# Zero products in TensorE's gaps, a weight's sign by Prelu, and a new order of work

## The chip, the cores and the metric

The kernel runs on one core of one Trainium2 chip. The metric is the device time of one execution in microseconds (us). Five engines work side by side: TensorE (products, PE in the profile, its weight loads PEld), VectorE (DVE), ScalarE (ACT), GpSimd (POOL) and SyncE (SP), whose queue issues the DMAs.

## The reference

Three stages follow one another. Linear attention over 4 batches, 8 heads, 576 tokens, head size 64, with 128 random features; an MLP of 512 - 2048 - 512 with a leaky ReLU; and an MLP of 512 - 1024 - 512 with a softmax-weighted product and a layer norm inside.

```python
def phi(x):
    proj = np.einsum('bhsd,md->bhsm', x, omega)
    h = proj - np.sum(x * x, axis=-1, keepdims=True) / 2.0
    h = h - np.max(h, axis=-1, keepdims=True)
    return np.exp(h) / np.sqrt(m)
q_p, k_p = phi(q * scale), phi(k * scale)
kv = np.einsum('bhsm,bhsd->bhmd', k_p, v);  z = np.sum(k_p, axis=2)
attn = einsum(q_p, kv) / (einsum(q_p, z) + 1e-06)      # -> x: 2304 tokens x 512
h = x @ w_in;   x = np.maximum(0.01 * h, h) @ w_out
h = x @ w2_in;  e = np.exp(h - h.max());  solu = h * e / e.sum()
out = ((solu - mean) / np.sqrt(var + 1e-06) * g_ln) @ w2_out
```

q, k, v and omega come as float32. The four weight matrices come as float64, so each element is two 32-bit words and the kernel must rebuild a float32 from them.

## The kernel before, in words

The 2304 tokens are 18 tiles of 128. For a tile of k (`k_unit`) the kernel loads the rows of all heads, transposes them, multiplies by omega, takes the maximum and the exponential, and adds the products with v to the batch's sum kv (two PSUM tiles, `kv0` and `kv1`, for even and odd heads). For a tile of q (`q_unit`) it computes the same features and multiplies them with kv of the batch. Two tiles make a block of 256 tokens for the first MLP: `st1` is its first layer (product at L1080 for the first block in float32, at L1086 for the others in split float16), `st2` its second (L1126 and L1130). `mlp2_in` (L1245), `mlp2_mid` and `mlp2_out` (L1319) are the second MLP.

A weight matrix comes in pieces of 128 x 512 float64 (`piece`, L359). Each has a buffer `wraw` (four of them), a DMA of 512 KB, and then: the high words scaled by 2^-112 into x (L378 on ScalarE, or L381 on POOL; the list `ya` says which), a shift left by three (L384, VectorE), the sign, and the three bits of the low word (L400, VectorE). The sign comes in one of two ways (list `sg`): a Sign on ScalarE (L393) and a product on POOL (L404), or a bit operation on VectorE (L397). The pieces of the first MLP are numbered 0 to 31 (w_in, then w_out), all of the second MLP have 99. Later a piece is cut into two float16 parts (`cut_weight`); the list `wlo` says which are cut with POOL's help.

The first block needs all pieces of w_in in order, four (a chunk) for each two of its eight groups; the cuts come when it is through with them.

The order of all instructions is chosen when the program is built. `Issue` (L28) is a planner: it steps through generators, each with a priority (the smaller, the earlier), and keeps a model of when each engine is free. An operation that is ready goes into its engine's heap; when the engine is free in the model, the operation with the smallest priority is taken and emitted. On the chip each engine then runs its instructions in this order. Buffers are counted: `get` waits for one, `put` gives it back; a waiting `get` is served by priority, but a buffer that is free goes to the first who asks. `X` holds the numbers of buffers, the priorities (`due` of each unit from `deadlines`, plus the offsets in `off`), and the lists that say which engine does what. A weight's load and work have the priority w1 + w1s * chunk (or w2 + w2s * row) + its offset.

`v_bound` reads the v of the last two batches once, at the start, to find a scale, and is started ahead of the units; `v_load` brings v for the sums. Both take a buffer `v`. `omega_prep` loads omega twice, one load after the other, and transposes it (L496).

`warm_up` (L476) is ten products of 512 columns of a zeroed tile at the start of TensorE's work, into a bank that a tile `y` has for this time.

Of the kernel before, what the change touches and what calls it, by code (L numbers as in the profile page):

```python
# [9 lines left out]
F32 = mybir.dt.float32  # L10
F16 = mybir.dt.float16
# [10 lines left out]

X = {'NF': 1, 'bufs': {'qe': 3, 'v': 2, 'qf': 2, 'ke': 4, 'hl': 1, 'x': 2, 'g': 4, 'sg': 1, 'qT': 3, 'x16': 3, 'scr': 2, 'T': 1, 'wraw': 4, 'raw': 1, 'y16': 2, 'lnT': 3, 'l16': 2, 'kf': 2, 'v16': 3}, 't0': -33.903, 'tb': 232.119, 'w1': -284.718, 'w1s': -136.489, 'w2': 138.823, 'w2s': 11.803, 'b0': -432.337, 'b1': 58.985, 'dk': 50.766, 'dq': -11.625, 'dl': 188.956, 'c1': -291.243, 'c2': -74.124, 'pw2': 106.795, 'wlo': [1, 4, 11, 12, 13, 15, 16, 20, 23, 24, 25, 27, 30, 32, 33, 35, 39], 'vd': 829.749, 'warm': 10, 'psq': ['k0', 'k4', 'q4', 'q7', 'q8'], 'ep': ['k1', 'k12', 'k14', 'k16', 'k3', 'k4', 'k5', 'k6', 'k7', 'q0', 'q1', 'q15'], 'te': ['k00', 'k01', 'k10', 'x00', 'x11'], 'KH': [2, 3], 'vb': 346.274, 'ya': [0, 3, 4, 5, 6, 7, 8, 9, 11, 12, 13, 15, 20, 21, 24, 25, 28, 29, 30, 31, 99], 'EK': [0, 1, 2, 3, 6, 7, 8], 'pkv': 346.335, 'tail': 3, 'sg': [1, 3, 9, 11, 13, 14, 18, 19, 20, 29], 'off': {'q1': -191.7, 'w15': 506.92, 'w4': 40.08, 'w23': -275.29, 'w18': -183.5, 'w24': 49.7, 'w28': -14.13, 'q10': 139.42, 'k8': -330.31, 'q5': 145.52, 'w7': 124.91, 'w25': -154.21, 'w12': -66.92, 'w9': -115.28, 'w19': -197.26, 'w31': 261.27, 'w27': -201.22, 'k11': 48.35, 'q16': -139.34, 'w5': 217.6, 'k9': 38.48, 'q2': 183.77, 'w8': 21.25, 'w14': -107.85, 'w30': 145.73, 'e1': 252.86, 'w26': -557.18, 'k13': -105.91, 'q0': 40.51, 'k0': 104.04, 'k7': 50.33, 'q13': 128.56, 'k2': -96.21, 'k16': -192.43, 'w22': 156.65, 'k6': 19.45, 'k4': 269.03, 'q8': 59.66, 'v0': 128.19, 'w20': -694.52, 'w16': 175.72, 'w0': 75.39, 'q6': 56.03, 'v2': -26.38, 'w17': 84.39, 'w13': 306.69, 'w3': 539.5, 'v1': 84.72, 'e2': -21.1, 'w1': -197.63, 'k15': -23.53, 'q3': 335.59, 'w2': 510.76, 'q7': 95.01, 'q4': 199.6, 'w11': 44.31, 'q12': 134.9, 'k5': 117.67, 'q15': -72.68, 'w10': 64.06, 'k14': -24.99, 'w29': 230.81, 'q17': -396.39, 'k12': 87.94, 'v3': -15.84, 'w21': -618.68, 'q11': 42.31, 'q9': 133.04, 'k17': 24.82, 'q14': -332.91, 'k1': 23.08, 'e3': -27.5, 'w6': 222.38, 'k3': 306.64, 'k10': -25.2}, 'pe': -72.358}


class Issue:  # L28
# [152 lines left out]
def linear_attention_moe_kernel(  # L181
# [177 lines left out]
    def piece(src, r0, c0, n, x, pool, nr):  # L359

        yield "get", "wraw"
        u = h = None
        if src.dtype == F32:
            yield "op", "DMA", 1.58, lambda: SP.dma_start(out=x, in_=src[r0:r0 + 128, c0:c0 + n])
        else:
            h = {}

            def load():
                h["r"] = mk(pool, "wraw", [128, n, 2], I32)
                SP.dma_start(out=h["r"].rearrange("p n w -> p (n w)"),  # L370
                             in_=src[r0:r0 + 128, c0:c0 + n].bitcast(I32))
            yield "op", "DMA", 1.58, load

            hw = lambda: h["r"][:, :, 1].bitcast(F32)
            xi = x.bitcast(I32)

            def base_A():
                yield "op", "A", 0.61, lambda: A.activation(out=x, in_=hw(), func=AF.Copy, scale=2.0 ** -112)  # L378

            def base_G():  # L380
                yield "op", "G", 0.75, lambda: G.tensor_scalar(out=x, in0=hw(), scalar1=2.0 ** -112, scalar2=1.0,  # L381
                                                               op0=ALU.mult, op1=ALU.mult)
            yield from either("ya", nr, base_A, base_G)
            yield "op", "V2", 0.38, lambda: V.tensor_scalar(out=xi, in0=xi, scalar1=3, scalar2=None,  # L384
                                                           op0=ALU.logical_shift_left)
            sg = {}

            def sign():
                yield "get", "sg"

                def emit():
                    sg["t"] = mk(pool, "sg", [128, n], F16)
                    A.activation(out=sg["t"], in_=hw(), func=AF.Sign)  # L393
                yield "op", "A", 0.6, emit, True

            def sign_bit():
                yield "op", "V2", 0.62, lambda: V.scalar_tensor_tensor(  # L397
                    out=xi, in0=h["r"][:, :, 1], scalar=-(1 << 31), in1=xi, op0=ALU.bitwise_and, op1=ALU.bitwise_or)
            yield from either("sg", nr, sign, sign_bit)
            yield "op", "V2", 0.62, lambda: V.scalar_tensor_tensor(  # L400
                out=xi, in0=h["r"][:, :, 0], scalar=29, in1=xi, op0=ALU.logical_shift_right, op1=ALU.bitwise_or)

            def signed():
                yield "op", "G", 1.2, lambda: G.tensor_tensor(out=x, in0=x, in1=sg["t"], op=ALU.mult)  # L404
                yield "put", "sg"
            yield from either("sg", nr, signed, lambda: ())
        yield "put", "wraw"

    def bound(pool, x, am, n, gain=1.0):
# [63 lines left out]
            yield "set", ("w2", f)  # L473


    def warm_up():  # L476

        yield "get", "y"
        ps = mk(ps_y, "y", [128, DM], F32)
        z = omT.rearrange("p a m -> p (a m)").bitcast(F16)  # L480
        for n in range(X["warm"]):
            yield "op", "PE", 0.215, lambda: PE.matmul(ps, lhsT=z[:, 0:128], rhs=z, start=True, stop=True), True
        yield "put", "y"

    def omega_prep():
        yield "get", "scr"
# [310 lines left out]
    def k_unit(i, pri):  # L797
# [14 lines left out]
        def half(hh):  # L812
# [12 lines left out]
                yield "wait", ("v", nv)  # L825
            for p, n, b in segs[i]:
                if (yield "nth", ("kv of", b), 1):
                    yield "get", "kv"
                    kv_ps[b] = [ps_kv.tile([128, HH, D + 2], F32, name=f"kv{g}", tag=f"kv{g}") for g in range(2)]
                    yield "set", ("kv at", b)  # L830
                    yield "end",
                yield "wait", ("kv at", b)

                def acc(p=p, n=n, b=b):
                    left["kv", b, hh] -= 1
                    first = left["kv", b, hh] == len(batch_segs[b]) - 1
# [583 lines left out]
```

## Time and profile before

| | us |
|---|---|
| median of 3 runs | 716.52 (715.64 to 718.06) |
| the profiled execution | 716.71 |
| its span, first to last instruction | 714.9 |
| mean granted clock of TensorE in it | 0.982 |

The profiled execution is the one whose rows are shown below. A row "8.00:10.00 2.00, ..." of a view by windows gives for a stretch the busy time of each engine and the count of its instructions, TensorE's granted clock, the busy share of the DMA engines and the GB/s that they moved. A clock of 1.00 is 2.4 GHz, 0.50 is 1.2 GHz. A float32 product of TensorE stands as two records.

### The profile page before, as it was taken

How to read it: one execution, taken by the hardware profiler on the slowest of the kernel's cores; microseconds unless marked ns; L12 is line 12 of the kernel's file. 1: busy time of each engine (PE TensorE's matmuls, PEld its weight loads, DVE VectorE, ACT ScalarE, POOL GpSimd, SP SyncE). 2: the span in 40 equal slices, each digit the busy share in tenths (PEclk: the TensorE clock that was granted, in tenths of full speed). 3: DMA queues.
4: the chain of work that ended last, by engine and by line, in shares of the span. 5: the costliest groups of instructions: out<-in, count | busy, mean ns of one | idle time of the engine just before them, and what ended most of it. 6: DMA issues, size and time to landing. Idle time of an engine off the chain costs nothing. (4 is left out here: it accounts for less than half of the span.)

```text
span 714.9 us, 12932 instructions
## 1 busy us (share of the span) xinstructions
PE 687.9 (96%) x4892; PEld 446.1 (62%) x4892; DVE 493.1 (69%) x1197; ACT 380.4 (53%) x801; POOL 128.0 (18%) x170
## 2 busy tenths in 40 slices
PE   4889989999999999999999999999999999999997
PEld 2878975577677667767677767566654444444443
DVE  5998989889676586765964426974068758668870
ACT  3888868698675766756565526876132121121121
POOL 3321332434210110011110000043001101101120
PEclk7878999999999999999999999999999999999999
DMA  9878786548665345453654516901015233333343
GB/s 281 242 241 284 191 227 141 111 89 163 98 126 89 56 83 115 83 98 73 120 98 66 85 26 219 270 9 30 1 31 91 72 89 72 82 69 74 69 106 76
DMA packets 183598, 81.19 MB, mean 114 GB/s; under 512 B 146416, under 2 KB 175088, under 8 KB 183536
## 3 DMA queue, kind: packets, MB, share of 16 engines
q1 hardware_dynamic: 183536, 80.37, 49.4%
q8 instruction: 38, 0.62, 0.3%
q14 instruction: 24, 0.20, 0.1%
HBM read 41.75 MB, written 4.72 MB: 65 GB/s over the span
## 5 line engine op out<-in xcount | busy, mean ns | idle before, releaser
L1130 PE MATMUL y<-w,g 128*128 128x512 f16 x768 | 177.6, 379 | 0.8 <-DVE g L1104 0.3
L1086 PEld LDWEIGHTS <-w 128*128 128x128 f16 x1536 | 148.6, 98 | 26.9 <-issue 0.6
L1130 PEld LDWEIGHTS <-g 128*128 128x128 f16 x768 | 72.9, 98 | 78.7 <-DVE g L1104 3.7
L1086 PE MATMUL h<-xy,w 128*128 128x256 f16 x960 | 112.3, 273 | 0.0
L1319 PE MATMUL h<-wo,lnT 128*128 128x512 f16 x432 | 95.8, 379 | 0.0
L1104 DVE TENSOR_TENSOR g<-h,g 128x512 f16<-128x512 f32 x64 | 43.8, 685 | 46.8 <-ACT g L1103 46.5
L1245 PE MATMUL h<-wi,xy 128*128 128x512 f16 x336 | 75.3, 379 | 0.0
L1319 PEld LDWEIGHTS <-lnT 128*128 128x128 f16 x432 | 42.3, 98 | 51.0
L1102 ACT ACTIVATE h<-h 128x512 f32<-128x512 f32 x64 | 38.1, 596 | 57.2 <-PE h L1086 57.1
L1086 PE MATMUL h<-xT,w 128*128 128x256 f16 x576 | 68.1, 273 | 0.0
L1274 ACT ACTIVATE e<-h,nb,u 128x1024 f32<-128x1024 f32 x18 | 21.7, 1205 | 74.8 <-DVE nb L1271 64.0
L1245 PEld LDWEIGHTS <-xy 128*128 128x128 f16 x336 | 32.9, 98 | 38.8
L783 ACT ACTIVATE qe<-a,nb,sc 128x128 f32<-128x128 f32 x120 | 44.6, 471 | 15.5 <-DVE nb L774 14.3
L1328 ACT ACTIVATE osb<-h,c_out 128x512 f32<-128x512 f32 x18 | 12.4, 687 | 68.2 <-PE h L1319 36.4
L768 DVE TENSOR_REDUCE mx<-a 128x4 f32<-128x512 f32 x63 | 41.7, 682 | 7.3 <-PE a L761 5.0
L869 POOL TENSOR_SCALAR qf<-qe 128x512 f16<-128x512 f32 x30 | 19.1, 637 | 121.7 <-ACT qe L783 116.0
L1103 ACT ACTIVATE g<-h 128x512 f16<-128x512 f32 x64 | 38.5, 602 | 1.1
L1289 POOL TENSOR_TENSOR rs<-ve,mhalf 128x1 f32<-128x1 f32 x18 | 9.9, 550 | 145.4 <-DVE ve L1288 145.4
L783 ACT ACTIVATE ke<-a,nb,sc 128x128 f32<-128x128 f32 x64 | 23.6, 468 | 17.2 <-DVE nb L774 9.9
L1080 PE MATMUL h<-xT,w 128*128 128x256 f32 x128 | 29.1, 382 | 2.2 <-ACT g L1099 2.2
L872 DVE SCALAR_TENSOR_TENSOR qf<-qe,qf 128x512 f16<-128x512 f32 x30 | 21.9, 729 | 13.6 <-POOL qf L869 13.4
L1126 PE MATMUL y<-w,g 128*128 128x512 f32 x64 | 29.5, 600 | 0.2 <-DVE w L400 0.2
(200 smaller groups left out, 1134.2 us busy)
## 6 DMA issues: line engine op xcount, KB each, us to landing
wraw<-in_moe_w_in_dram SPq DMA_DIRECT2D x24, 512.0 KB, 5.7
wraw<-in_moe_w_out_dram SPq DMA_DIRECT2D x24, 512.0 KB, 4.4
v<-in_v_dram SPq DMA_DIRECT2D x12, 512.0 KB, 5.7
raw<-in_k_dram SPq DMA_DIRECT2D x8, 512.0 KB, 4.6
raw<-in_q_dram SPq DMA_DIRECT2D x8, 512.0 KB, 5.0
out_dram<-osb SPq DMA_DIRECT2D x16, 256.0 KB, 2.2
v<-in_v_dram SPq DMA_DIRECT2D x6, 128.0 KB, 5.1
lnT<-l SPq DMA_TRANSPOSE x36, 3.2
```

What stands on the lines that cost most here:

```text
L768: yield "op", "V", 0.6, lambda: V.tensor_reduce(out=u["mx"][:, hh::2], in_=w["ps"], axis=AX.X, op=ALU.max)
L783: A.activation(out=x[:, h, :], in_=w["ps"][:, h, :], func=AF.Exp, scale=st["sc"], bias=u["nb"][:, 2 * h + hh:2 * h + hh + 1])
L872: yield "op", "V" if stay else "V2", 0.62, lambda: V.scalar_tensor_tensor(out=w["f"][:, :, 1, :], in0=w["e"], scalar=2.0 ** 14, in1=w["f"] ...
L1080: PE.matmul(ps[:, f, :], lhsT=stash(w1, c * KC + kc)[:, o:o + 128], rhs=xT[j][:, kc, :], start=(kc == 0), stop=(kc == KC - 1))
L1086: PE.matmul(ps[:, f, :], lhsT=w1[:, c * KC + kc, w, o:o + 128], rhs=xT[j][:, :, xo + kc, :], start=(n == 0), stop=(n == 3 * KC - 1))
L1102: yield "op", "A", 0.48, lambda: A.activation(out=ps, in_=ps, func=AF.Prelu, scale=2.0 ** -19, alpha=0.01)
L1103: yield "op", "A", 0.48, lambda: A.activation(out=gg[:, 0], in_=ps, func=AF.Copy)
L1104: yield "op", "V", 0.6, lambda: V.tensor_tensor(out=gg[:, 1], in0=ps, in1=gg[:, 0], op=ALU.subtract)
L1126: PE.matmul(y_ps[j][t], lhsT=gg[:, f, ts], rhs=stash(w2, 2 * p + f), start=(ends[0] and f == 0), stop=(ends[1] and f == 1))
L1130: PE.matmul(y_ps[j][t], lhsT=gg[:, a, f, ts], rhs=w2[:, 2 * p + f, w, :], start=(ends[0] and f == 0 and n == 0), stop=(ends[1] and f == 1 ...
L1245: PE.matmul(ps[:, f, :], lhsT=yT[i][:, a + c, :], rhs=W["i"][:, 2 * c + f, w, :], start=(j == 0 and c == 0), stop=(j == 2 and c == KC - 1))
L1319: PE.matmul(ps, lhsT=t[:, a, f, :], rhs=W["o"][:, f, w, :], start=(j == 0 and f == 0), stop=(j == 2 and f == KF2 - 1))
```

## The change

- `X` is new: priorities, offsets, buffers and lists. Of the buffers, v goes from 2 to 1, g 4 to 9, ke 4 to 3, kf 2 to 4, qT 3 to 2, x16 3 to 2, y16 2 to 3, lnT 3 to 2. The last tiles of the second MLP that go ahead of its output layer are 5 instead of 3 (`tail`).
- The list `sg` is gone. Pieces in `ya` (22 of 32) get x and sign in one Prelu on ScalarE; for a negative number its slope of -2^32 sets an exponent bit that the shift by three moves to the sign's place. The others, the second MLP's among them, are scaled on POOL and get the sign by the bit operation on VectorE.
- `warm_up` is now up to 300 products of 128 columns of zeros, with the largest priority number of all, so that one is emitted when nothing else is ready for TensorE in the model. They go to 128 added columns of the tile `kv1`, and stop when the tiles of the attention are all done.

```diff
-X = {... 'bufs': {'qe': 3, 'v': 2, ... 'ke': 4, ... 'g': 4, ... 'lnT': 3, ...}, ... 'w1': -284.718, ... 'w2': 138.823, ... 'warm': 10, ... 'tail': 3, 'sg': [1, 3, 9, 11, 13, 14, 18, 19, 20, 29], ...}
+X = {... 'bufs': {'qe': 3, 'v': 1, ... 'ke': 3, ... 'g': 9, ... 'lnT': 2, ...}, ... 'w1': 54.105, ... 'w2': 352.332, ... 'warm': 300, ... 'tail': 5, ...}
+    nil = const.tile([128, 128], F16, name="nil")
-            yield from either("ya", nr, base_A, base_G)
-            yield "op", "V2", 0.38, lambda: V.tensor_scalar(out=xi, in0=xi, scalar1=3, ...
+            def sign_A():
+                yield "op", "A", 0.63, lambda: A.activation(out=x, in_=hw(), func=AF.Prelu, scale=2.0 ** -112,
+                                                            alpha=-2.0 ** 32)
+                yield from shift()
+            def sign_V():
+                yield "op", "G", 0.75, lambda: G.tensor_scalar(out=x, in0=hw(), scalar1=2.0 ** -112, scalar2=1.0,
+                                                               op0=ALU.mult, op1=ALU.mult)
+                yield from shift()
                 yield "op", "V2", 0.62, lambda: V.scalar_tensor_tensor(
                     out=xi, in0=h["r"][:, :, 1], scalar=-(1 << 31), in1=xi, op0=ALU.bitwise_and, op1=ALU.bitwise_or)
-            yield from either("sg", nr, sign, sign_bit)
+            yield from either("ya", nr, sign_A, sign_V)
...
-                yield "op", "G", 1.2, lambda: G.tensor_tensor(out=x, in0=x, in1=sg["t"], op=ALU.mult)
...
+    idle = []
+    def kv_place(b):
+        ps = [ps_kv.tile([128, HH * (D + 2) + 128], F32, name=f"kv{g}", tag=f"kv{g}") for g in range(2)]
+        kv_ps[b] = [p[:, 0:HH * (D + 2)].rearrange("p (h d) -> p h d", h=HH) for p in ps]
+        idle.append(ps[1][:, HH * (D + 2):])
+
     def warm_up():
-        yield "get", "y"
-        ps = mk(ps_y, "y", [128, DM], F32)
-        z = omT.rearrange("p a m -> p (a m)").bitcast(F16)
+        yield "get", "kv"
+        kv_place(0)
         for n in range(X["warm"]):
-            yield "op", "PE", 0.215, lambda: PE.matmul(ps, lhsT=z[:, 0:128], rhs=z, start=True, stop=True), True
-        yield "put", "y"
+            if not idle:
+                break
+            def zeros(n=n):
+                if idle:
+                    PE.matmul(idle[-1], lhsT=nil, rhs=nil, start=n == 0, stop=False, skip_group_check=True)
+            yield "op", "PE", 0.1, zeros, True
...
+        idle.clear()
...
-        sch.go(warm_up(), -101)
+        sch.go(warm_up(), 1e8)
```

## Rows read from the trace of the kernel before

**Rows 1.** The page's first part: busy us (share of the span) x instructions.
```profile
PE 687.9 (96%) x4892; PEld 446.1 (62%) x4892; DVE 493.1 (69%) x1197; ACT 380.4 (53%) x801; POOL 128.0 (18%) x170
```
**Rows 2.** Windows by stage: busy us (x count) by engine, clock, DMA share, GB/s.
```profile
0.00:70.95 70.95, 54.06 (x349) 47.79 (x350) 57.76 (x132) 50.14 (x118) 18.17 (x28) 0.83 0.87 262
20.00:50.60 30.60, 26.60 (x189) 24.89 (x187) 29.65 (x66) 26.67 (x69) 7.70 (x8) 0.89 0.81 238
70.95:710.50 639.55, 633.84 (x4545) 398.36 (x4543) 435.36 (x1067) 329.62 (x683) 109.79 (x142) 1.00 0.46 98
710.50:714.90 4.40, 0.00 (x0) 0.00 (x0) 0.00 (x0) 0.68 (x1) 0.00 (x0) 0.78 0.26 60
```
**Rows 3.** Waits of TensorE: us in total, times, longest us.
```profile
PE h L496 <- DMA scr<-in_omega_dram: 8.6, 1, 8.6
```
**Rows 4.** Windows of two us in the first stretch, columns as in rows 2.
```profile
8.00:10.00 2.00, 0.00 (x0) 0.00 (x0) 1.97 (x6) 1.22 (x2) 0.00 (x0) 0.96 1.12 348
...
18.00:20.00 2.00, 2.00 (x11) 2.00 (x11) 1.23 (x2) 0.31 (x1) 2.00 (x3) 0.50 1.08 311
...
52.00:54.00 2.00, 2.00 (x8) 1.47 (x9) 1.89 (x6) 2.00 (x8) 0.00 (x0) 0.50 0.81 237
```
**Rows 5.** Timeline of TensorE: start, us, line, out<-in, shape, count, wait before.
```profile
1.17 4.45 PE L482 MATMUL y<-omT 128*128 128x512 f16 x10 [1.17 <-DVE omT L1365]
5.41 1.54 PE L729 MATMUL h<-ident,raw 128*128 128x128 f32 x8
...
38.74 1.92 PE L757 MATMUL a<-omT,T 128*128 128x128 f32 x8
...
45.03 1.11 PE L757 MATMUL a<-omT,T 128*128 128x128 f32 x8
...
90.35 0.22 PE L760 MATMUL a<-omA,T 128*128 128x128 f16 x1
90.41 0.22 PE L761 MATMUL a<-omB,T 128*128 128x128 f16 x1
```
**Rows 6.** Groups of instructions before 70.95 us: busy us, mean ns, idle before.
```profile
L400 DVE SCALAR_TENSOR_TENSOR w<-wraw,w 128x512 int32<-128x512 int32 x19 | 12.9, 681 | 0.0
...
L404 POOL TENSOR_TENSOR w<-w,sg 128x512 f32<-128x512 f32 x7 | 8.8, 1252 | 18.6 <-DVE w L400 9.3 <-DVE mh L772 7.6 <-ACT ke L783 1.7
L397 DVE SCALAR_TENSOR_TENSOR w<-wraw,w 128x512 int32<-128x512 int32 x12 | 8.2, 681 | 0.1
...
L381 POOL TENSOR_SCALAR w<-wraw 128x512 f32<-128x512 f32 x8 | 5.5, 687 | 25.0 <-DMA wraw<-in_moe_w_out_dram 24.9
```
**Rows 7.** Timeline of SyncE's queue: two issues near the start.
```profile
4.91 0.68 SPq L244 DMA_DIRECT2D v<-in_v_dram  x1
5.64 3.11 SPq L493 DMA_DIRECT2D scr<-in_omega_dram  x1
```
**Rows 8.** Timeline of VectorE and POOL about 21 to 25 us.
```profile
21.52 0.16 DVE L774 SCALAR_TENSOR_TENSOR nb<-mh,sq 128x8 f32<-128x8 f32 x1
...
23.63 1.28 POOL L404 TENSOR_TENSOR w<-w,sg 128x512 f32<-128x512 f32 x1 [3.35 <-DVE mh L772]
...
23.81 1.12 DVE L774 SCALAR_TENSOR_TENSOR nb<-mh,sq 128x8 f32<-128x8 f32 x1
```
**Rows 9.** Window of the second MLP's weights, columns as in rows 2.
```profile
428.00:460.00 32.00, 32.00 (x230) 22.33 (x229) 23.91 (x52) 22.04 (x50) 0.00 (x0) 1.00 0.81 239
```
**Rows 10.** DMA issues: count, KB each, median us from issue to landing.
```profile
v<-in_v_dram SPq DMA_DIRECT2D x12, 512.0 KB, 5.7
...
lnT<-l SPq DMA_TRANSPOSE x36, 3.2
```
**Rows 11.** Timeline: the first batch's last kv product and ScalarE's read of kv.
```profile
48.31 2.25 PE L846 MATMUL kv<-v,ke 128*128 128x65 f32 x16 [1.28 <-ACT ke L783]
...
55.52 0.76 ACT L886 ACTIVATE kv<-kv 128x256 f32<-128x256 f32 x2
```
**Rows 12.** Timeline of TensorE at the end: the last five output tiles.
```profile
684.34 26.06 PE L1319 MATMUL h<-wo,lnT 128*128 128x512 f16 x120
```

More of the change, by code (lines that the diff above doesn't have):

```diff
@@ L16 @@
 PSUM = bass.MemoryType.PSUM
-X = {'NF': 1, 'bufs': {'qe': 3, 'v': 2, 'qf': 2, 'ke': 4, 'hl': 1, 'x': 2, 'g': 4, 'sg': 1, 'qT': 3, 'x16': 3, 'scr': 2, 'T': 1, 'wraw': 4, 'raw': 1, 'y16': 2, 'lnT': 3, 'l16': 2, 'kf': 2, 'v16': 3}, 't0': -33.903, 'tb': 232.119, 'w1': -284.718, 'w1s': -136.489, 'w2': 138.823, 'w2s': 11.803, 'b0': -432.337, 'b1': 58.985, 'dk': 50.766, 'dq': -11.625, 'dl': 188.956, 'c1': -291.243, 'c2': -74.124, 'pw2': 106.795, 'wlo': [1, 4, 11, 12, 13, 15, 16, 20, 23, 24, 25, 27, 30, 32, 33, 35, 39], 'vd': 829.749, 'warm': 10, 'psq': ['k0', 'k4', 'q4', 'q7', 'q8'], 'ep': ['k1', 'k12', 'k14', 'k16', 'k3', 'k4', 'k5', 'k6', 'k7', 'q0', 'q1', 'q15'], 'te': ['k00', 'k01', 'k10', 'x00', 'x11'], 'KH': [2, 3], 'vb': 346.274, 'ya': [0, 3, 4, 5, 6, 7, 8, 9, 11, 12, 13, 15, 20, 21, 24, 25, 28, 29, 30, 31, 99], 'EK': [0, 1, 2, 3, 6, 7, 8], 'pkv': 346.335, 'tail': 3, 'sg': [1, 3, 9, 11, 13, 14, 18, 19, 20, 29], 'off': {'q1': -191.7, 'w15': 506.92, 'w4': 40.08, 'w23': -275.29, 'w18': -183.5, 'w24': 49.7, 'w28': -14.13, 'q10': 139.42, 'k8': -330.31, 'q5': 145.52, 'w7': 124.91, 'w25': -154.21, 'w12': -66.92, 'w9': -115.28, 'w19': -197.26, 'w31': 261.27, 'w27': -201.22, 'k11': 48.35, 'q16': -139.34, 'w5': 217.6, 'k9': 38.48, 'q2': 183.77, 'w8': 21.25, 'w14': -107.85, 'w30': 145.73, 'e1': 252.86, 'w26': -557.18, 'k13': -105.91, 'q0': 40.51, 'k0': 104.04, 'k7': 50.33, 'q13': 128.56, 'k2': -96.21, 'k16': -192.43, 'w22': 156.65, 'k6': 19.45, 'k4': 269.03, 'q8': 59.66, 'v0': 128.19, 'w20': -694.52, 'w16': 175.72, 'w0': 75.39, 'q6': 56.03, 'v2': -26.38, 'w17': 84.39, 'w13': 306.69, 'w3': 539.5, 'v1': 84.72, 'e2': -21.1, 'w1': -197.63, 'k15': -23.53, 'q3': 335.59, 'w2': 510.76, 'q7': 95.01, 'q4': 199.6, 'w11': 44.31, 'q12': 134.9, 'k5': 117.67, 'q15': -72.68, 'w10': 64.06, 'k14': -24.99, 'w29': 230.81, 'q17': -396.39, 'k12': 87.94, 'v3': -15.84, 'w21': -618.68, 'q11': 42.31, 'q9': 133.04, 'k17': 24.82, 'q14': -332.91, 'k1': 23.08, 'e3': -27.5, 'w6': 222.38, 'k3': 306.64, 'k10': -25.2}, 'pe': -72.358}
@@ new lines @@
+X = {'NF': 1, 'bufs': {'qe': 3, 'v': 1, 'qf': 2, 'ke': 3, 'hl': 1, 'x': 2, 'g': 9, 'sg': 1, 'qT': 2, 'x16': 2, 'scr': 2, 'T': 1, 'wraw': 4, 'raw': 1, 'y16': 3, 'lnT': 2, 'l16': 2, 'kf': 4, 'v16': 3}, 't0': 38.107, 'tb': 187.479, 'w1': 54.105, 'w1s': -59.238, 'w2': 352.332, 'w2s': 14.253, 'b0': -113.048, 'b1': -6.038, 'dk': 42.281, 'dq': 74.634, 'dl': 206.254, 'c1': -41.937, 'c2': -59.523, 'pw2': 104.035, 'wlo': [1, 3, 8, 11, 13, 14, 16, 17, 25, 28, 31, 34, 36, 37, 38, 39], 'vd': 105.739, 'warm': 300, 'psq': ['k0', 'q0', 'q3', 'k6', 'q6', 'q7', 'q8', 'q9'], 'ep': ['k1', 'k12', 'k14', 'k16', 'k3', 'k4', 'k5', 'k6', 'k7', 'q0', 'q1'], 'te': ['k00', 'k01', 'k11', 'k40', 'k41', 'x10', 'x11'], 'KH': [2, 3], 'vb': 118.863, 'ya': [0, 1, 4, 6, 7, 9, 11, 12, 13, 14, 15, 16, 17, 18, 19, 20, 22, 23, 24, 27, 29, 31], 'EK': [0, 1, 2, 3, 6, 7, 8], 'pkv': 56.661, 'tail': 5, 'off': {'q1': -150.9, 'w15': 261.17, 'w4': 14.2, 'w23': -532.04, 'w18': 143.18, 'w24': -228.68, 'w28': 52.21, 'q10': 208.4, 'k8': -54.41, 'q5': 362.46, 'w7': 254.87, 'w25': 296.88, 'w12': 299.75, 'w9': -116.63, 'w19': 106.43, 'w31': 120.17, 'w27': -435.77, 'k11': -354.41, 'q16': -125.64, 'w5': 228.93, 'k9': -15.0, 'q2': 245.68, 'w8': 98.43, 'w14': -147.85, 'w30': -294.84, 'e1': 30.87, 'w26': 198.68, 'k13': 18.32, 'q0': 10.8, 'k0': -175.63, 'k7': 93.8, 'q13': 199.99, 'k2': -2.3, 'k16': -339.39, 'w22': -96.81, 'k6': -286.1, 'k4': 122.7, 'q8': 12.64, 'v0': -2.93, 'w20': -418.66, 'w16': 175.2, 'w0': 352.98, 'q6': 324.81, 'v2': 1.52, 'w17': -233.24, 'w13': 60.91, 'w3': -282.06, 'v1': 51.23, 'e2': 80.0, 'w1': 21.19, 'k15': -13.38, 'q3': -61.35, 'w2': -459.82, 'q7': 171.44, 'q4': 93.37, 'w11': 210.27, 'q12': -65.87, 'k5': 105.62, 'q15': 86.28, 'w10': 85.38, 'k14': -4.24, 'w29': -114.4, 'q17': -227.35, 'k12': -171.67, 'v3': 295.13, 'w21': -21.91, 'q11': -31.65, 'q9': 12.76, 'k17': 83.15, 'q14': 50.45, 'k1': 72.93, 'e3': 132.73, 'w6': -32.87, 'k3': -224.59, 'k10': 456.53}, 'pe': -535.604}
@@ L375, in piece, with shift @@
             xi = x.bitcast(I32)
-            def base_A():
-                yield "op", "A", 0.61, lambda: A.activation(out=x, in_=hw(), func=AF.Copy, scale=2.0 ** -112)
-            def base_G():
+            def shift():
+                yield "op", "V2", 0.38, lambda: V.tensor_scalar(out=xi, in0=xi, scalar1=3, scalar2=None,
+                                                               op0=ALU.logical_shift_left)
+            def sign_A():
[3 more added lines that the diff above has]
+            def sign_V():
                 yield "op", "G", 0.75, lambda: G.tensor_scalar(out=x, in0=hw(), scalar1=2.0 ** -112, scalar2=1.0,
                                                                op0=ALU.mult, op1=ALU.mult)
-            yield from either("ya", nr, base_A, base_G)
[L384 to L396, printed above, removed]
+                yield from shift()
                 yield "op", "V2", 0.62, lambda: V.scalar_tensor_tensor(
                     out=xi, in0=h["r"][:, :, 1], scalar=-(1 << 31), in1=xi, op0=ALU.bitwise_and, op1=ALU.bitwise_or)
-            yield from either("sg", nr, sign, sign_bit)
+            yield from either("ya", nr, sign_A, sign_V)
             yield "op", "V2", 0.62, lambda: V.scalar_tensor_tensor(
                 out=xi, in0=h["r"][:, :, 0], scalar=29, in1=xi, op0=ALU.logical_shift_right, op1=ALU.bitwise_or)
-            def signed():
-                yield "op", "G", 1.2, lambda: G.tensor_tensor(out=x, in0=x, in1=sg["t"], op=ALU.mult)
-                yield "put", "sg"
-            yield from either("sg", nr, signed, lambda: ())
         yield "put", "wraw"
@@ L827, in half @@
                 if (yield "nth", ("kv of", b), 1):
-                    yield "get", "kv"
-                    kv_ps[b] = [ps_kv.tile([128, HH, D + 2], F32, name=f"kv{g}", tag=f"kv{g}") for g in range(2)]
+                    if b:
+                        yield "get", "kv"
+                        kv_place(b)
                     yield "set", ("kv at", b)
@@ L1365, in linear_attention_moe_kernel @@
         V.memset(omT, 0.0)
+        V.memset(nil, 0.0)
         for vt in v_ring:
```

## The prediction, made before the changed kernel was run

> **What bounds the kernel now.** I read the page's first part for who is busiest, then the busy time by stage, then what TensorE waits for, then the first 70 us more finely. The reader is to see first that TensorE is busy 687.9 of 714.9 us [rows 1], so at most 27 us of idleness can go, besides time at the lower clock. The stages say where both lie. From 70.95 us, when the first layer of the first MLP starts, to 710.5 us TensorE is busy 633.84 of 639.55 us at clock 1.00: 5.7 us idle in 640 [rows 2]. The change takes no product out of that stretch, so it can win little there. Up to 70.95 us it is busy 54.06 us at a mean clock of 0.83, and the last 4.4 us are the last store [rows 2]. What can be won lies in the first 71 us.
>
> Three things fill that stretch. First, the longest wait of TensorE in the whole run: 8.6 us, until omega has landed [rows 3]. Second, the clock. After that wait it is at half: 0.96 in the two us from 8, 0.50 from 18 and again 0.50 from 52 [rows 4]. Eight records of the projection (four products) take 1.92 us at half and 1.11 at full [rows 5]; seven such groups fall into the three half-clock stretches, so 7 x 0.81 = 5.7 us. Third, VectorE: between 20 and 50.6 us it is busy 29.65 of 30.6 us, more than TensorE's 26.60 [rows 2]. It makes TensorE's operands and, between them, rebuilds weight pieces; the last step of a piece stands 19 times before 70.95 us [rows 6].
>
> Useful work at full clock in this stretch is 54.06 - 4.45 (the ten warm-up products [rows 5]) - 5.7 = 43.9 us. So 27 us of the 71 do nothing useful.
>
> **The change part by part.**
>
> *Omega.* At the start the queue issues what holds a buffer, in order of priority; omega's second load, at 5.64 us, stands behind two loads of v, the later at 4.91 us [rows 7]. With one v buffer instead of two, the bound of v (started first) takes it, so only one load of v stands ahead. A load of 512 KB at the 311 to 348 GB/s of these windows [rows 4] takes 1.5 to 1.7 us. Gain 1.5 to 1.7; I take 1.6.
>
> *Products of zeros.* The ten of 512 columns become up to 300 of 128 columns, placed where the planner's TensorE has nothing ready, until the attention is over. A 128-column f16 product follows another by 0.06 us [rows 5]; at half clock a quarter of the old warm-up's 4.45 / 10 gives 0.11. All 300 in the way would cost 18 to 33 us; all in real gaps, nothing. The gaps of the first stretch alone are 16.9 us, plus the old warm-up's 4.45. Each is planned at 0.1 us, longer than its 0.06 at full clock, so they fit in planned gaps; where the chip's gaps lie elsewhere some delay a real product. I take 0.5 us. In return the clock should stay up: the ten zero products at the start ran at half pace (the clock column has no change yet there) and were followed by eight 128-column records in 1.54 us, between the 1.11 and 1.92 us that eight take at either clock [rows 5]: the clock rose behind zeros, the only sight of it here. Gain 0 to 5.7 us; since VectorE is as full in the same time, a faster product is partly a longer wait: I take 4.
>
> *The sign by Prelu.* Of the 32 pieces of the first MLP, ten took a Sign on ScalarE and a product on POOL (L404), 22 a bit operation on VectorE (L397). Now 22 get the sign in the ScalarE pass that they need anyway, through a negative slope that puts a bit where the shift by three moves it to the sign; ten keep the bit operation. By the sorted priorities the 20 first pieces hold five of these ten, against 12 L397 before 70.95 us [rows 6]: 7 x 0.68 = 4.8 us less on VectorE. The seven signed products of the stretch [rows 6] go as well, and they hold VectorE: a two-input operation of 0.16 us took 1.12 beside one that ran 1.28 [rows 8]. That is 0 to 7 x 0.96 = 6.7 us; I take 3.4. Two more copies of transposes move to VectorE: + 2 x 0.69, by L397's length, as the trace of a copy is as wide. Net 6.8 us less, half of it on the path, since TensorE is the later one in part of the stretch: gain 3.4, between 0 and 6.8. A Prelu pass itself costs what L378's copy did, which it replaces: nothing.
>
> *The second MLP's 16 pieces* go from ScalarE's scaling to POOL's, 0.69 us each [rows 6], 11 us on an engine that is idle from 428 to 460 us, where TensorE is busy 32.00 of 32 us [rows 9]: nothing, unless POOL holds VectorE for as long, and then those weights come 11 us later behind work that covers it.
>
> *Order.* Before, weight pieces (priorities down to -802) compete with the first batches' units; now all k and q units of the first batch and most of the second come first (-1325 to -419), the weights after (-406 up). That should bring the first two token tiles earlier. Bounds: with omega at some 14 us and 1.5 us of transposes before, 12.5 of the 27 us are unavoidable; beyond the terms above it can win 27 - 12.5 - 9 = some 5, and lose what the rival below costs. I take 0.
>
> *Buffers.* v in one buffer means that each pair of tiles waits for the pair before, then 5.7 us for its load [rows 10]. The first batch needs three in series; before, its last product began at 48.31 us [rows 11]. From about 21 us, three times (4 us of products + 5.7) ends at 50: no later, with projections to do meanwhile. Nine g instead of four, three y16: only slack. Two lnT instead of three: two transposes, the second landing 3.2 us after issue [rows 10], must fit into one output tile, 26.06 / 5 = 5.2 us [rows 12], and some 4.5 do. Between 0 and 3 us at the end; I take 0.5.
>
> *The bank.* The zeros go into unused columns of the tile of the second kv sum. In the run before, VectorE and ScalarE read the first batch's kv from the end of its last product, 50.56 us, to 56.28 us [rows 11]. If a zero is ordered behind such a read, TensorE stands behind it. Price 0 to 5.7 us; TensorE had real work there, so few zeros should stand there: I take 0.
>
> The Trainium skill speaks against me here: "PSUM — Partial Sum Buffer", in "PSUM bank collisions raise a hardware error", says that accesses of two engines are to be kept apart by bank, not by address. By that rule the unused columns are no protection, and a zero waits for the reads of its bank; the sum would be 5.7 us worse. No row here shows a product beside a reader of its bank.
>
> **Sum.** -1.6 - 4 - 3.4 + 0.5 + 0.5 = -8.0 us on the profiled execution's 716.71 us (span 714.9 and 1.8 around it), so 708.7. The median of the three runs, 716.52, lies 0.2 lower: 708.5.
>
> **Rivals.**
>
> 1. *VectorE and the latencies stay the bound.* The zeros keep the clock up, but every product then waits for VectorE, and the signed products had hidden behind waits. For it: 29.65 of 30.6 us busy. Against it: VectorE itself loses work. Left: omega's 1.6 and a little: 713.5 to 716.
>
> 2. *Zeros wait for the readers of kv.* One such wait gives 708.5 + 5.7 = 714. For it: the shared bank; against it: TensorE's own work at that time.
>
> 3. *Weights come late: slower.* The place is the second chunk of the first layer, two groups (7.2 us) after that layer starts. With the new priorities its last piece is about the twentieth. Pieces came at (70.95 - 10.3) / 19 = 3.2 us each (the first ends at 10.3); at that rate the twentieth stands at 71 to 74 us, against a need at 62 + 7 = 69, and second-batch attention of TensorE (about 10 us by the same groups) covers it. If attention's precedence slows pieces to 4.4 us, it stands at 94: 25 late, 10 covered, 15 lost against 8 gained: 723. It decides from 4.1 us a piece. Against it: VectorE has less to do for a piece.
>
> 4. *The order wins its 5 us too*: 703 or less.
>
> **How the numbers follow.** Forecast (703 to 713) 0.58; below 703, 0.08; rival 1, 0.14; rival 2, 0.07; rival 3, 0.13. A difference of 0.3% (2.1 us) is about what can be told from none. Faster: 0.58 + 0.08 and, of rivals 1 and 2, 0.05 + 0.04 = 0.75. Same: the rest of these two, less 0.01 beyond: 0.11. Slower: 0.14. The range 698 to 718 leaves out rival 3 and a few in a hundred below.
>
> **What would show it.** Right: the first L1080 product of the changed kernel at 60 to 65 us instead of 70.95; granted clock 1.00 from about 10 us to the end; no L404 rows and some ten L397 for the first MLP; omega's products near 14 us; 634 +- 3 us busy of TensorE from the first L1080 to the end of products. Wrong: half-clock stretches between zeros, waits of TensorE for kv's readers, an L1080 that waits for weights (rebuilt w), or more than 8 us of idleness after the first L1080.

## The result and the profile after

Timed on one chip, four executions each: 708.69 us (707.77 to 710.29) after, 717.29 us (715.64 to 718.07) before; ratio 0.990, 95% interval 0.988 to 0.992. The change makes the kernel 1.0% faster; the forecast was 708.5. The profiled execution took 708.97 us, its span is 707.2 us, 7.7 less than before's 714.9, and the mean granted clock in it 0.998 (before 0.982).

The page's first part for the kernel after, to set beside [rows 1]: busy us (share of the span) x instructions.

```profile
PE 692.8 (98%) x5162; PEld 457.2 (65%) x5162; DVE 481.4 (68%) x1191; ACT 361.5 (51%) x770; POOL 132.8 (19%) x177
```

Windows by stage of the kernel after, columns as in [rows 2]. The first product of the first layer (L1084, before L1080) divides them:

```profile
0.00:66.70 66.70, 58.59 (x573) 56.37 (x573) 52.64 (x145) 44.34 (x109) 7.82 (x16) 0.97 0.82 251
66.70:702.80 636.10, 634.16 (x4592) 400.82 (x4590) 428.78 (x1047) 316.52 (x662) 125.00 (x161) 1.00 0.46 101
702.80:707.20 4.40, 0.00 (x0) 0.00 (x0) 0.00 (x0) 0.64 (x1) 0.00 (x0) 1.00 0.26 60
20.00:50.00 30.00, 27.73 (x263) 27.06 (x264) 24.42 (x65) 19.51 (x56) 3.21 (x3) 0.94 0.90 260
```

The first stretch is 4.25 us shorter (66.70 against 70.95), the second 3.45 (636.10 against 639.55), the last store as long as it was. The clock of the first stretch rose from 0.83 to 0.97. VectorE, which was busy 29.65 of 30.6 us in the middle of it, is now busy 24.42 of 30.

The busy time of TensorE now holds zeros, so it can't be set beside the one before. The same view for the products of zeros alone (L485):

```profile
0.00:66.70 66.70, 16.52 (x215) 14.92 (x215) 0.97 0.82 251
...
110.00:702.80 592.80, 6.52 (x55) 4.47 (x55) 1.00 0.43 92
```

280 of the 300 were run, 215 of them before the first layer; the remaining ten lie between 66.7 and 110 us.

Where TensorE's time goes: the kernel after by two-us windows (beside [rows 4]), its waits (us in total, times, longest; beside [rows 3]) and its timeline (beside [rows 5]).

```profile
8.00:10.00 2.00, 2.00 (x37) 2.00 (x35) 2.00 (x6) 0.68 (x1) 0.60 (x1) 1.00 0.98 300
18.00:20.00 2.00, 1.44 (x19) 1.08 (x15) 2.00 (x7) 2.00 (x8) 0.00 (x0) 1.00 1.08 389
46.00:48.00 2.00, 2.00 (x11) 2.00 (x10) 1.20 (x4) 2.00 (x4) 0.00 (x0) 0.50 0.94 352
52.00:54.00 2.00, 1.94 (x17) 1.86 (x16) 1.71 (x5) 1.99 (x7) 0.00 (x0) 1.00 0.15 26
```
```profile
PE kv L850 <- DMA v<-in_v_dram: 2.6, 3, 1.6
...
PE h L499 <- DMA scr<-in_omega_dram: 1.2, 1, 1.2
PE kv L485 <- ACT kv L890: 0.9, 1, 0.9
```
```profile
7.61 3.93 PE L485 MATMUL kv<-nil 128*128 128x128 f16 x62
...
12.77 0.30 PE L499 MATMUL h<-ident,scr 128*128 128x128 f32 x1 [1.23 <-DMA scr<-in_omega_dram]
13.45 1.16 PE L760 MATMUL a<-omT,T 128*128 128x128 f32 x8
...
43.15 2.00 PE L850 MATMUL kv<-v,ke 64*128 64x65 f32 x16 [1.60 <-DMA v<-in_v_dram]
...
66.70 3.62 PE L1084 MATMUL h<-xT,w 128*128 128x256 f32 x16
```

The reader is to see: 62 zeros from 7.61 us fill what was the wait for omega, and the clock stands at 1.00 at 8 and at 18 us; one stretch at half is left, around 46 us, behind a wait of 1.60 us for v that ends at 43.15; and omega's product starts at 12.77 us. Before, it started at 15.5 (the eight records of 1.54 us from 5.41 end at 6.95 [rows 5], then 8.6 us [rows 3]).

VectorE's groups of the kernel after before 66.7 us (busy us, mean ns, idle before; beside [rows 6] and [rows 8]):

```profile
L396 DVE SCALAR_TENSOR_TENSOR w<-wraw,w 128x512 int32<-128x512 int32 x18 | 12.5, 708 | 0.0
...
L393 DVE SCALAR_TENSOR_TENSOR w<-wraw,w 128x512 int32<-128x512 int32 x5 | 3.3, 684 | 0.0
L777 DVE SCALAR_TENSOR_TENSOR nb<-mh,sq 128x8 f32<-128x8 f32 x8 | 1.3, 157 | 0.0
```

There are five sign bits (L393) instead of twelve. The short two-input step of which [rows 8] shows one held up for 1.12 us beside POOL's signed product runs freely: L777's eight take 157 ns each in the mean. Before, seven of them took 569 ns each:

```profile
L774 DVE SCALAR_TENSOR_TENSOR nb<-mh,sq 128x8 f32<-128x8 f32 x7 | 4.0, 569 | 0.0
```

### The profile page after: what moved, and what is told of

The parts are those of the page before. It is cut to its first block, busy times and chain, and to the rows that moved or that the text cites. A ratio compares the mean times of both kernels' runs of the same rounds, so it can differ in the third digit from the quotient of the medians.

```text
span 707.2 us, 13423 instructions
## 1 busy us (share of the span) xinstructions
PE 692.8 (98%) x5162; PEld 457.2 (65%) x5162; DVE 481.4 (68%) x1191; ACT 361.5 (51%) x770; POOL 132.8 (19%) x177
## 4 chain that ended last, share of the span: by engine, by line
PE 75%; issue 7%; DMA 6%; ACT 5%; DVE 4%; POOL 1%; SPq 0%; POOLq 0%; ACTq 0%; DVEq 0%
PE h L1090 17%; PE y L1134 16%; PE h L1324 13%; PE h L1250 13%; DMA v<-in_v_dram 4%; PE h L1084 4%; PE kv L850 3%; ACT qe L786 2%; PE y L1130 1%; PE a L1008 1%; DVE mx L771 1%; PE a L763 1%; PE a L764 1%; DMA qT<-qf 1%; ACT ke L786 1%
## 5 line engine op out<-in xcount | busy, mean ns | idle before, releaser
L1324 PE MATMUL h<-wo,lnT 128*128 128x512 f16 x432 | 96.0, 379 | 0.0
L1324 PEld LDWEIGHTS <-lnT 128*128 128x128 f16 x432 | 42.3, 98 | 51.0
L786 ACT ACTIVATE qe<-a,nb,sc 128x128 f32<-128x128 f32 x128 | 47.1, 468 | 15.2 <-DVE nb L777 13.8
L876 DVE SCALAR_TENSOR_TENSOR qf<-qe,qf 128x512 f16<-128x512 f32 x32 | 23.6, 738 | 16.0 <-POOL qf L873 16.0
L672 POOL TENSOR_TENSOR scr<-raw 128x1024 f32<-128x1024 f32 (+1 forms) x8 | 14.4, 1801 | 91.1 <-DMA raw<-in_q_dram 80.8
L1274 DVE TENSOR_REDUCE mx<-h 128x1 f32<-128x1024 f32 x18 | 21.9, 1216 | 12.1 <-PE h L1250 12.1
```

The source lines that it names most:

```text
L786: A.activation(out=x[:, h, :], in_=w["ps"][:, h, :], func=AF.Exp, scale=st["sc"], bias=u["nb"][:, 2 * h + hh:2 * h + hh + 1])
L876: yield "op", "V" if stay else "V2", 0.62, lambda: V.scalar_tensor_tensor(out=w["f"][:, :, 1, :], in0=w["e"], scalar=2.0 ** 14, in1=w["f"] ...
L1274: yield "op", "V", 1.13, lambda: V.tensor_reduce(out=mx, in_=ps, axis=AX.X, op=ALU.max)
L1324: PE.matmul(ps, lhsT=t[:, a, f, :], rhs=W["o"][:, f, w, :], start=(j == 0 and f == 0), stop=(j == 2 and f == KF2 - 1))
```

## Experiments

Three groups of runs, each timed against the kernel before on one chip, as ratios with a 95% interval. The theory to begin with was the prediction's: the clock, the sign and omega's load each bring some us. The rival: one of them brings all, and the others are hidden.

**The kernel after, again, and without its zeros.** The second leaves only the zeros out; order, buffers and the wait for the tile stay.

```diff
-                if idle:
+                if idle and n < 0:
```

> The changed kernel once more, on the chip of the next three runs, as what they are measured against. By its four runs so far: 707.8 to 710.3 us, some 0.990 of the kernel before.

> The changed kernel, every other instruction in the same order on every engine, but none of its 280 products of zeros. My theory (the zeros hold the clock and that is worth about 4 us, since a faster product is partly a longer wait): 712 to 714 us, half-clock stretches in at least two places before the first layer of the first MLP, which starts 3 to 5 us later than 66.7. Rival 1 (VectorE and latencies are the bound, the clock is hidden): at most 710 us, although the clock falls as before. Rival 2 (zeros also hold TensorE up, behind readers of kv): faster than 708.

The kernel after again: 0.9904 (0.9877 to 0.9932), 710.78 us, its first layer at 68.13 us and its mean clock up to there 0.95; so that start varies by over a us between two profiled executions. Without zeros: 0.9898 (0.9873 to 0.9923), 710.18 us. Windows of the kernel without zeros, the first eight records of its projections, and one of its waits:

```profile
0.00:69.10 69.10, 52.16 (x357) 48.29 (x358) 51.95 (x145) 44.15 (x109) 7.79 (x16) 0.93 0.77 241
35.00:40.00 5.00, 5.00 (x31) 5.00 (x30) 2.58 (x5) 3.43 (x12) 1.89 (x1) 0.62 1.07 329
40.00:45.00 5.00, 4.90 (x29) 4.36 (x29) 2.72 (x7) 2.31 (x4) 1.31 (x2) 0.70 0.92 272
69.10:703.10 634.00, 630.80 (x4527) 396.64 (x4525) 427.41 (x1048) 316.89 (x662) 124.78 (x161) 1.00 0.47 101
```
```profile
13.96 2.07 PE L760 MATMUL a<-omT,T 128*128 128x128 f32 x8 [0.38 <-DVE omT L502]
```
```profile
PE kv L850 <- ACT kv L890: 0.9, 1, 0.9
```

The clock falls again where the zeros had held it (0.62 and 0.70 from 35 to 45 us, behind a wait of 1.59 us for v that ends at 34.68). It was low earlier too: the column still reads 1.00 at 14 us, but eight records take 2.07 us there, the pace of the half clock [rows 5], against 1.16 with zeros. So the mean of 0.93 is too high for this run. The first layer starts 1 to 2.4 us later than in the two profiles with zeros. But from there to the end of products it takes 634.0 us against 636.1, and the whole is the same. The theory (712 to 714 us) missed; rival 1, the hidden clock (at most 710), fits but for 0.2 us. The zeros raise the clock and are worth nothing that can be measured; the two intervals leave some 2.7 us either way.

**Fewer zeros** (`n < 92` and `n < 215` in the same line): is a part of them useful and another part in the way?

> The changed kernel in the same order, with only the first 92 zeros, which all lie before omega has landed; the later 188 are left out. If the long wait for omega is the gap that costs the clock, this is within 1 us of the changed kernel (708 to 710) with the clock at 1.00 up to 40 us. If the many short gaps between 17 and 52 us need their zeros too, the clock falls in two places there and the time is 711 to 713.

> The changed kernel in the same order with its first 215 zeros, those ahead of the first layer of the first MLP; the last 65 are left out. New theory (zeros win 1 to 2.4 us before the first layer by the clock, and the 65 behind it lie in the way of a full TensorE at 0.056 us each, 3.6 us): 2 to 3.6 us faster than the changed kernel, 707 to 708.5 here, first layer from 66.7 to 68.2 us, 634 us from there to the last product. Rival (zeros change nothing anywhere; the shorter second part without any zeros was chance): 710 to 711.

0.9909 (0.9884 to 0.9935) and 0.9906 (0.9887 to 0.9925), 710.86 and 710.03 us. Neither: the late zeros cost nothing either. With the first 92 alone the clock, expected at 1.00 up to 40 us, fell to 0.83 from 10 to 20 us and to 0.59 from 35 to 40, and the time stayed. Without the late ones the stretch behind the first layer takes 635.68 us, with TensorE busy for 630.92 of them, so the late zeros had mostly filled gaps. Why that stretch is the shortest without any zeros stays open.

**The old load of the sign put back into the new order.** Behind the shift of each of 13 Prelu pieces stands the sign bit again, which changes nothing there, and behind the last step of the nine others that were in `sg` a pass of POOL with two inputs (zeros added). ScalarE's Sign is not put back. `POOLED` is before's list `sg`; the cut is shortened.

```diff
 def shift_more():
     V.tensor_scalar(out=xi, in0=xi, scalar1=3, ...)
+    if nr not in POOLED:
+        V.scalar_tensor_tensor(out=xi, in0=h["r"][:, :, 1], scalar=-(1 << 31), in1=xi, ...)
...
 def low():
     V.scalar_tensor_tensor(out=xi, in0=h["r"][:, :, 0], scalar=29, ...)
+    if nr in POOLED and nr in X["ya"]:
+        G.tensor_tensor(out=x, in0=x, in1=nil (broadcast), op=ALU.add)
```

> The changed kernel in the same order, with VectorE and POOL made to carry what the old way to the sign cost them: 13 of the 22 Prelu pieces get the bit operation on VectorE as well (it sets a bit that is set already), the other 9 a two-input pass on POOL that adds zeros. Only the Sign on ScalarE is not put back. My theory (6.8 us of VectorE's time in the first stretch, half of it on the path): 711 to 713, first layer 3 to 4 us later. Rival (VectorE has slack for it in the new order): within 1 us of the changed kernel.

1.0019 (0.9998 to 1.0040), 717.93 us: the whole gain is gone, which is more than the theory had (711 to 713) and the opposite of the rival. Windows of this kernel, its POOL group (whole run), and one of VectorE (before 72.55 us):

```profile
0.00:72.55 72.55, 62.02 (x572) 59.72 (x573) 59.78 (x153) 44.73 (x109) 14.64 (x22) 0.93 0.78 234
...
72.55:711.60 639.05, 635.94 (x4592) 401.38 (x4590) 434.14 (x1053) 316.89 (x662) 130.42 (x164) 1.00 0.46 100
```
```profile
L409 POOL TENSOR_TENSOR w<-w,nil 128x512 f32<-128x512 f32 x9 | 10.6, 1180 | 48.9 <-DVE den L1029 21.8 <-DVE w L406 18.9 <-DVE nb L791 7.2
```
```profile
L791 DVE SCALAR_TENSOR_TENSOR nb<-mh,sq 128x8 f32<-128x8 f32 x8 | 2.2, 273 | 0.0
```

VectorE is busy 59.78 us ahead of the first layer instead of 52.64, and some of its short operations are stretched again (273 ns in the mean against 157, though not the 569 of the kernel before). The first layer comes at 72.55 us, 5.85 later than in the first profile of the kernel after and 4.42 later than in the second, and the stretch behind it is 639.05 us long, close to the 639.55 from before the change.

The two halves of that load, each by itself:

> The changed kernel in the same order, with only the 13 bit operations put back on VectorE (each sets a bit that is set already). Both together, with 9 passes on POOL, cost 7.2 us. Theory (VectorE's time is the path until the weights are done, so 13 x 0.68 = 8.9 us more of it costs 5 to 7): 715.5 to 717. Rival (POOL's passes, which hold VectorE, cost most): at most 713.

> The changed kernel in the same order, with only the 9 two-input passes of zeros put back on POOL. Theory as for the run with the 13 operations: 711 to 713 here. Rival (POOL's passes hold VectorE by 0.96 us each, 8.6 in all, and the maxima of a chunk wait for them): 715 to 717.

VectorE's 13 bits alone: 0.9958 (0.9935 to 0.9980), 713.8 us, between its theory and its rival. POOL's nine passes alone: 0.9931 (0.9910 to 0.9952), 711.47 us, as its theory had it. The same short step of VectorE, before the first layer, with the bits alone and then with POOL's passes alone:

```profile
L788 DVE SCALAR_TENSOR_TENSOR nb<-mh,sq 128x8 f32<-128x8 f32 x8 | 1.3, 158 | 0.0
```
```profile
L788 DVE SCALAR_TENSOR_TENSOR nb<-mh,sq 128x8 f32<-128x8 f32 x8 | 2.2, 272 | 0.0
```

So it is POOL's passes that stretch it. Against 0.9906 of the run beside them (its late zeros alone left out) that is 0.5% (3.7 us) and 0.25% (1.8 us); both together take the ratio from 0.9904 to 1.0019, 8.2 us (7.2 by the medians). By these middles VectorE's own work is the larger part, but each difference is uncertain by some 2 us (2.5 for both together): POOL's part is not clear of nothing, and whether the two are worth more together than one by one can't be told.

**The sign alone in the kernel before, order chosen anew.** Before's numbers with Prelu pieces; the planner makes its order for them.

```diff
-            yield from either("ya", nr, base_A, base_G)
...
+            yield from either("ya", nr, sign_A, sign_V)
```

> The kernel before with one thing of the change alone: the sign by Prelu, with the changed kernel's list of which pieces take it; priorities, buffers and the warm-up of ten products are the old ones, and the planner makes an order from them. If the sign is the whole gain: 709 to 711. If it takes the new order to turn VectorE's time into TensorE's: 714 to 717.

1.0454 (1.0430 to 1.0478), 749.3 us. The first layer starts at 89.11 us. Work was taken away, and the kernel is 32 us slower. The planner made another order, with priorities that were chosen for other work, and the new list also moves other pieces, and the second MLP's, to POOL. The run measures all that together, and tells nothing about the sign.

**The sign alone, in place.** So the next one keeps every other instruction of before where it stood, and leaves out of before's order, for the 20 pieces of the first MLP in its `ya`, 14 sign bits, 6 Signs and 6 signed products of POOL:

```diff
+                    if nr < 32:
+                        A.activation(out=x, in_=hw(), func=AF.Prelu, scale=2.0 ** -112, alpha=-2.0 ** 32)
...
-                yield "op", "V2", 0.62, lambda: V.scalar_tensor_tensor(
+                yield "op", "V2", 0.62, lambda: done or V.scalar_tensor_tensor(
...
-                yield "op", "G", 1.2, lambda: G.tensor_tensor(out=x, ...
+                yield "op", "G", 1.2, lambda: done or G.tensor_tensor(out=x, ...
```

> The kernel before, in its own order, with the sign by Prelu put in place: the 20 pieces of the first MLP that ScalarE scales take Prelu in that pass, and their later sign steps (14 bit operations on VectorE; 6 Signs on ScalarE and 6 products on POOL) are left out where they stood. Theory now (VectorE's time until the weights are rebuilt is what counts: 14 x 0.68 + 6 x 0.96 = 15 us less of it, where 17.5 us more cost the changed kernel 7.2): 6 us faster, 710 to 712.5. Rival (only the new order can use it): 715 to 717.

1.0001 (0.9986 to 1.0015), 717.04 us, twelve executions: nothing, as the rival had it (the theory was 710 to 712.5). Windows of its profiled execution (718.82 us, the longest of the twelve, so its lengths are not compared), its timeline, and the same products for q in the timeline of the kernel before:

```profile
20.00:50.00 30.00, 24.05 (x165) 22.68 (x164) 21.09 (x54) 19.72 (x51) 3.10 (x3) 0.84 0.86 232
...
33.00:41.50 8.50, 5.94 (x38) 5.71 (x37) 4.89 (x15) 2.41 (x6) 1.16 (x1) 0.80 0.98 197
```
```profile
33.18 0.38 SPq L244 DMA_DIRECT2D raw<-in_q_dram  x1
33.61 1.23 SPq L527 DMA_TRANSPOSE omA<-hl  x1
...
36.67 1.15 SPq L527 DMA_TRANSPOSE omB<-hl  x1
...
41.48 1.06 PE L737 MATMUL h<-ident,raw 128*128 128x128 f32 x8 [2.56 <-DMA raw<-in_q_dram]
42.52 1.22 DVE L669 TENSOR_REDUCE sq<-scr 128x16 f32<-128x1024 f32 x1 [3.98 <-ACT scr L673]
```
```profile
41.41 1.04 PE L729 MATMUL h<-ident,raw 128*128 128x128 f32 x8
```

VectorE was indeed relieved, 21.09 us busy in 30 against 29.65 in 30.6 [rows 2], and what it got free became waiting. The timeline shows one place: the rows of q, issued at 33.18 us, are used at 41.48, with the DMA engines busy 0.98 of the time between and TensorE, VectorE and ScalarE all idle at its end. The kernel before uses these rows at 41.41, without a wait: what the lighter VectorE had won up to there ends in that wait.

**Omega's second load, issued right behind the first**, in the kernel before, there with the sign in place as well, and in the kernel after without zeros:

```diff
-            yield "op", "DMA", 0.2, lambda c=c: SP.dma_start(out=om2[:, c], in_=omega)
+            yield "op", "DMA", 0.2, lambda c=c: [SP.dma_start(out=om2[:, j], in_=omega) for j in range(2) if c == 0]
```

> The kernel before, in its own order, with one move: omega's second load of 32 KB is issued right behind its first, ahead of a load of weights and one of v, so that it lands some 5 us earlier. If the wait of 8.6 us for omega is on the path: 712 to 715, since VectorE is idle 3.5 us of the 10 from 10 us on. If VectorE, full from 20 us, sets the pace anyway: 716.5 to 717.5.

> The kernel before in its own order with both: Prelu in place and omega's second load behind the first. If the two act on the same thing (VectorE's backlog in the first 70 us), their gains add: the sum of the two single runs' gains within 1.5 us, and with 6 and 3 us this would be 708. If omega's wait is the later of two waits in the same place, the sum falls short by most of the smaller one.

> The changed kernel in its order, without any zeros (710.2 without, 710.8 with them), and with omega's second load right behind its first. VectorE is busy 9.78 of the 10 us from 10 us on there, so little is to be had by the theory: 709 to 710.5. If omega's landing at 12.8 us still starts the chain that ends last: 706 to 708, and this is then the fastest of all.

0.9993 (0.9978 to 1.0008), 0.9986 (0.9964 to 1.0008) and 0.9908 (0.9889 to 0.9926); in us 716.32, 715.79 and 710.62. Waits of TensorE in the kernel before with omega early, and its VectorE in order of time:

```profile
PE a L757 <- DVE omT L499: 7.0, 1, 7.0
...
PE h L496 <- DMA scr<-in_omega_dram: 1.6, 1, 1.6
```
```profile
10.31 1.29 DVE L400 SCALAR_TENSOR_TENSOR w<-wraw,w 128x512 int32<-128x512 int32 x2
13.26 0.43 DVE L384 TENSOR_SCALAR w<-w 128x512 int32<-128x512 int32 x1 [1.66 <-POOL w L381]
...
15.33 0.58 DVE L499 TENSOR_SCALAR omT<-h 64x128 f32<-64x128 f32 x2
```

The wait of [rows 3] is gone (8.6 to 1.6 us) and stands one step later, 7.0 us: the transposed omega is ready at 8.9 us, and its copy to SBUF (L499) comes at 15.33, since VectorE's order has nine steps of weight pieces in front, with a wait of 1.66 us for POOL among them. With the sign in place that wait is 6.4 us; in the new order, 4.6. None of these kernels beats the kernel after, and the first two do not differ from the kernel before. The run with both (sign and omega) shows a second thing. Its TensorE does not wait for the rows of q, and uses them at 41.00 us. Its window from 33 us:

```profile
33.00:41.50 8.50, 8.50 (x47) 8.38 (x47) 4.40 (x12) 2.70 (x5) 1.18 (x1) 0.59 0.97 226
```

TensorE is busy for all of it at a clock of 0.59, while VectorE is busy for half of it.

## Why the prediction was right, and where it was not

The total came out (708.69 against 708.5) by luck: wrong terms cancelled. The gain forecast was 8.0 us; measured were 8.6 in the first runs and 6.5 in the run again (710.78 against 717.30). One line from TensorE's waits in the kernel before, after the start of its first layer, is needed below:

```profile
PE h L1080 <- ACT g L1099: 2.2, 2, 1.5
```

Step by step:

- **The place.** The gain was to lie in the first 71 us, with little to win behind. The span's 7.7 us are 4.25 there and 3.45 behind, where next to nothing was expected (the first layer was to start at 60 to 65 us; it started at 66.7 and 68.1). Part of the second is the first in disguise: ahead of the first layer TensorE now has 112 records of products with v for kv (two to a product) instead of 96. In the run without zeros TensorE works 630.80 us behind that point, not 633.84 [rows 2], 3.0 less, and idles 3.2 us, not 5.7. Of before's idle time there, 2.2 us are the two waits above, of the first layer for ScalarE's read of its products; no kernel in the new order has them. What took them away was not tested.
- **Zeros and clock, -4 +0.5: failed.** The mechanism is there (0.83 to 0.97), its worth is not: without them the ratio is 0.9898, with them 0.9904. The step that failed is "partly a longer wait: I take 4". It is the whole, as far as can be measured; rival 1 was right for this term. Two signs of being wrong came, both small: a half-clock stretch between zeros (46 us) and a wait for a reader of kv (0.9 us). The Trainium skill, "TensorE: Matmul & The Clock Gate", section "Why this matters for your kernels", wants TensorE kept busy so that it stays at the high clock. The trace agrees on the clock (0.50 at 18 us before, 1.00 after), and the runs add that the time need not follow.
- **The sign, -3.4, bounds 0 to 6.8: mis-sized.** In the new order it is worth 7 to 8 us (0.9904 to 1.0019, uncertain by 2.5), about the upper bound. The counts were right (5 sign bits against 12, no signed products), and a Prelu pass takes 700 ns where the copy took 706. "Half of it on the path" was too little: with 7.1 us more of VectorE's busy time ahead of the first layer, that layer starts 4.4 to 5.85 us later, and 2 to 3 us more are lost behind it, where the prediction put nothing. Put in before's own order the lighter sign is worth nothing (1.0001).
- **Order, 0.** By itself nothing that can be told: with the old load put back, the new order stands at 1.0019. But without it the lighter pieces bring nothing. The gain belongs to the pair, and a sum of terms, each priced alone, can't show that.
- **Omega, -1.6.** Its product starts 2.8 us earlier, by the mechanism named. Alone it is worth nothing that can be told (0.9993, 0.9978 to 1.0008): in either order an earlier load only moves the wait to VectorE's copy.
- **The bank of kv, 0 with 5.7 as its price: right.** One zero waits 0.9 us for ScalarE's read of kv (L890). In the run without zeros a product for kv waits 0.9 us for the same read, so the zero delayed nothing. Whether that wait is one of the bank or one written into the program for the tile, no run here tells. Rival 2 fell.
- **Weights late: fell.** No wait of the first layer for rebuilt weights is among TensorE's longest.
- **The rest, +0.5:** the last stretch is 4.40 us before and after, and the last products (L1319, now L1324) wait for nothing in either; there is nothing to see of lnT or of the tail.

Why the old order could not use a lighter VectorE is argued, not shown. The DMAs up to the first layer, of the kernel before and of the kernel after:

```profile
DMA packets 18314, 18.57 MB, mean 262 GB/s; under 512 B 3257, under 2 KB 15479, under 8 KB 18309
...
v<-in_v_dram SPq DMA_DIRECT2D x7, 512.0 KB, 5.9
wraw<-in_moe_w_out_dram SPq DMA_DIRECT2D x7, 512.0 KB, 5.2
```
```profile
DMA packets 15175, 16.73 MB, mean 251 GB/s; under 512 B 3200, under 2 KB 12416, under 8 KB 15169
...
wraw<-in_moe_w_out_dram SPq DMA_DIRECT2D x6, 512.0 KB, 6.8
v<-in_v_dram SPq DMA_DIRECT2D x4, 512.0 KB, 7.0
```

The old order issues three more loads of v and one more weight piece ahead of the first layer, and moves 1.84 MB more there: 7 us at its 262 GB/s. So two limits may lie close together in it: VectorE's work, and transfers in that order. Taking away the first alone would leave the second, as around the late q in the sign in place, with its 0.98 of DMA time; with fewer loads ahead and the old VectorE work, VectorE would limit. This would make both halves worth nothing alone. Against transfers as the only second limit stands the run with sign and omega: TensorE does not wait for q there, and the time is no better (0.9986). There TensorE itself is full at a clock of 0.59, so the low clock is a rival for the second limit in the old order; yet the new order without zeros has half-clock stretches too and keeps its gain. No run took the early loads of v out of the old order, or held the clock up in it with the lighter sign, so it stays open, as does the worth of the new order with its loads as before.

## What to carry to other kernels

Where each engine has a fixed order, work taken off the busiest one may pay only in an order that was chosen for the lighter work, as here (nothing in the old order, 7 to 8 us in the new); price the two as one. To test a part, leave its instructions out in place: a new order from old priorities measures the planner (749 us), not the part. A higher clock on TensorE bought no time here (0.95 and 0.97 with zeros against 0.93 without, ahead of the first layer, at equal ratios): before filling gaps, look whether the operands come from an engine that is the later one.

## What was not expected of the hardware

- 62 products of 128 columns of zeros, 63 ns apart, stand in for 3.93 us of the wait for omega, and the records behind them run at the full pace (eight in 1.16 us at 13.45, against 2.07 at 13.96 without zeros). They do not always hold it: behind 27 zeros and a wait of 1.60 us for v the clock reads 0.50 at 46 us.
- The clock column can read 1.00 where the products run at half pace (at 14 us without zeros): read the pace of like products beside it.
- A pass of POOL with two inputs stretches a short operation of VectorE with two inputs: 272 ns in the mean with nine such passes, 158 without, in the same order.
- A DMA share of 0.98 need not mean much data: 197 GB/s from 33 to 41.5 us with the sign in place, against 339 GB/s at 1.06 from 10 to 20 us of the kernel after. Two DMA transposes are issued in the first (33.61 and 36.67 us); that they are the reason was not tested.
